# A two-MLP kernel: one VectorE pass less in the first activation, the second MLP's weight decoding spread over the first, block sums moved to VectorE

## Chip, cores and metric

The kernel runs on one core of a Trainium2 chip (trn2). The metric is the device time of one execution in microseconds (us), lower is better; the median of several runs is given where there are several. The engines are TensorE (PE in the rows, its weight loads PEld), VectorE (DVE), ScalarE (ACT), GpSimd (POOL) and SyncE (SP), which here only issues DMAs.

## What is computed

Attention over x and 32 state rows per head gives 544 rows for each of 8 batches, 4352 rows of 512 (64 x 8 heads). They go through two MLPs, each 512 to 2048 to 512. The weights arrive as float64, the rest as float32.

```python
def _moe_ref(x, w_in, w_out):            # first MLP
    h = x @ w_in
    g = np.where(h >= 1, h, np.where(h <= -1, 0.0, (h + 1) ** 2 / 4))
    return g @ w_out

def _moe2_ref(x, w_in, w_out, alpha):    # second MLP
    h = x @ w_in
    g = np.maximum(h, 0.0) + alpha * np.minimum(h, 0.0)
    return g @ w_out
```

## The kernel before

**Weights.** TensorE multiplies in float32 or in a rounded format (fp32r). A float32 operand is split into a rounded high part and the rest as a low part, and a product is three matmuls (high x high, high x low, low x high; `mm3`, and the loops of `out_mm`, `h_item`, `o_item`). The high part is a ScalarE copy (`hi_`, L73), the low part a subtraction (`lo_`, L76), on VectorE unless an engine is named. A float64 weight tile (512 KB) is loaded as raw words by `d_load` (L302) into a buffer of pool V and turned to float32 by integer work: `dec0` is one ScalarE operation (L309), `dec1` four VectorE operations (L318, L320, L323, L326), the last of which frees the V buffer. Pool V has 10 buffers of 4 KB a partition, pool U has 80 of 2 KB, and PSUM has 4 banks for accumulators and 4 for everything else.

**First MLP.** Nine tiles of columns: tiles 0 to 7 are the 512 rows of x of a batch, tile 8 (256 wide) the state rows. Each tile has 16 steps, one for each 128 hidden features, so `steps` has 144 entries and `gi(t, f)` numbers them. At step i the list `side[i]` (filled by `at`) holds the other work that is written there: attention of the next batch, loads, decoding. The main loop takes `g_split(i + 1)`, the side work, `h_mm(i + 2)` and `act_fn(i + 2)` together, one piece of each in turn (`run`), then `out_mm(i)`. The weights of the first layer differ by tile: `vr_load` (L426) fetches those of the next tile, two steps ahead of `vr_hi`. Tile 8 takes the plain weights, which `w1s_load` (L450) fetches in 32 transfers of 256 KB.

**Activation.** `act_fn` has ScalarE write y = relu(h/2 + 1/2) from PSUM (L488), VectorE g = max(h, y) from PSUM (L489), then in a later piece VectorE g = min(y, 1) * g (L491). The PSUM bank of h is free after L489.

**Second MLP.** `second()` runs units q of 7 products (`h_item`, L668): block sums of activations and weights replace 8 products by 7. `w_sums` (L569) makes four sums of weight blocks a unit, `w_split` their high and low parts, `h_after` and `slope` (L693, L679) combine the products and apply the activation on VectorE and ScalarE. From the 36th product on, an output item (`o_split`, `o_item`, L733) stands after about every 1.75 products; its weights `wv` are loaded by `wo_get` (L653). `x_prep` builds the sums and splits of the activations for the next group of rows along one unit in eight; its low parts are half on GpSimd. GpSimd also runs `w_sums`, two of the four low parts in `w_split`, every second low part of `o_split`, and the low part of `w2o_put`.

**Second MLP's weights.** The 16 input tiles (`w2i`) are loaded, decoded and stored again (`w2i_store`, L548) from step `gi(6, 8)` on, one each 1.2 steps. The 16 output tiles (`w2o`) are decoded inside `second()`: the dictionary `later` places load, `dec0`, `dec1`, `w2o_put` (split) and `w2o_store` (L607) by product number, one tile each 1.75 products from product 24 on.

**Order.** The code's order gives priorities; a scheduler then fixes one order of instructions for each engine, and each engine (and SP's queue of DMAs) works through its own strictly in order, waiting where an input or a free buffer is not there yet.

Of the kernel before, what the change touches and what calls it, by code (L numbers as in the profile page):

```python
# [13 lines left out]
AF = mybir.ActivationFunctionType  # L14
# [26 lines left out]
def kernel_body(ctx: ExitStack, tc: tile.TileContext, x, state, w1i, w1o, w2i, w2o, alpha, out):  # L41
# [440 lines left out]
    def act_fn(i):  # L482
        n = wd_(steps[i][0])
        ps = HP.pop(i)[:, :n]
        g = U(f"g{i}")
        GG[i] = g
        y = U(f"y{i}")
        act.activation(out=y[:, :n], in_=ps, func=AF.Relu, bias=0.5, scale=0.5)  # L488
        dve.tensor_tensor(out=g[:, :n], in0=ps, in1=y[:, :n], op=ALU.max)  # L489
        yield  # L490
        dve.scalar_tensor_tensor(out=g[:, :n], in0=y[:, :n], scalar=1.0, in1=g[:, :n],  # L491
                                 op0=ALU.min, op1=ALU.mult)

# [66 lines left out]
    def w_sums(q):  # L560
# [6 lines left out]
        for o, a, b, op in ((s1, a21, a22, ALU.add), (s2, s1, a11, ALU.subtract),  # L567
                            (s3, a11, a21, ALU.subtract), (s4, a12, s2, ALU.subtract)):
            pool.tensor_tensor(out=o, in0=a, in1=b, op=op)  # L569
            yield  # L570

    def w_split(q, n):
# [9 lines left out]
        yield  # L582
        lo_(l, t, h, pool if n % 2 else dve)
        if n == 0:
# [11 lines left out]
    def w2o_put(n):  # L596

        raw = G.pop(("dec", ("w2o", FO[n])))
        h, l = U(f"woh{n}", F32R), U(f"wol{n}", F32R)
        hi_(h, raw)  # L600
        WR["o", n] = h, l
        yield
        lo_(l, raw, h, pool)

# [108 lines left out]
    def o_split(m):  # L713
# [5 lines left out]
        hi_(h, g)  # L719
        lo_(l, g, h, pool if m % 2 else dve)  # L720
        GS[m] = (h, l)
# [30 lines left out]
    def second():  # L752
# [7 lines left out]
        for kind, n in ev:  # L760
            if kind == "h":
                q, k = divmod(n, 7)
                h_item(n)
                h_after(n)
                todo = later.pop(n, [])
                if k == 0 and q + 2 < NL // 7:
# [89 lines left out]

    for n in range(16):
        key = ("w2i", n // 2, n % 2)
        o = gi(6, 8) + int(1.2 * n)
        at(o - 3, d_load, key, src_w2p(*key[1:]))  # L860
        decode(key, o)
        at(o + 5, w2i_store, *key[1:])
    later = defaultdict(list)
    for n, f in enumerate(FO):
        key = ("w2o", f)
        o = 24 + int(1.75 * n)
        later[o - 6].append((d_load, key, src_w2o(f)))
        later[o - 1].append((dec0, key))
        later[o].append((dec1, key))
        later[o + 2].append((w2o_put, n))  # L870
        later[o + 5].append((w2o_store, n))
    for k in range(4):
# [90 lines left out]
```

## Time and profile before

| what | value |
|---|---|
| median of 3 runs | 1567.62 us (1563.13 to 1568.17) |
| the profiled execution | 1563.17 us |
| its span, first to last instruction | 1561.4 us |
| mean granted TensorE clock | 0.961 |
| PE / DVE / ACT / POOL busy | 1442.1 / 1050.0 / 692.6 / 469.7 us |

The span is the time between the first and the last instruction; 1.8 us of the execution lie around it. Busy time of an engine is the time in which it had an instruction; the share of the span hides that the program has stages with different limits, so it is read stage by stage. A low granted clock follows where TensorE has been waiting.

### The profile page before, as it was taken

Reading aid. Unit: us, or ns where it says so; the run is one execution under the profiler, and the core shown is the slowest. Engines: PE = TensorE matmul, PEld = TensorE weight load, DVE = VectorE, ACT = ScalarE, POOL = GpSimd, SP = SyncE. Lnnn points to the kernel's source line nnn. Section 1 sums busy time; section 2 is a strip of 40 time slices with the busy share of each in tenths; the row PEclk is TensorE's granted clock in tenths of the full one; section 3 lists DMA queues with packets and bytes.
Section 4 is the critical chain, followed back from the end, with each engine's and each line's share of the span. In section 5 each row is a group of like instructions: output and inputs, shape, how many; then the busy total and the mean of one; then the engine's idle time right before and its main releaser. Section 6 shows DMA issues by size and latency. Waiting matters only on the chain.

```text
span 1561.4 us, 19131 instructions
## 1 busy us (share of the span) xinstructions
PE 1442.1 (92%) x6460; PEld 1182.7 (76%) x6460; DVE 1050.0 (67%) x1697; ACT 692.6 (44%) x1354; POOL 469.7 (30%) x461
## 2 busy tenths in 40 slices
PE   4599999999999999995797899999999999999997
PEld 2255688888888888785775677888788888878886
DVE  7798597868696879863379987445644665575530
ACT  3244565555544545432244444333434443444431
POOL 1112101121000000001255566434544554464521
PEclk8899999999999999997898999999999999999999
DMA  8999725565412214643334755344544554645554
GB/s 239 290 286 317 228 75 149 151 189 162 154 50 88 83 66 145 222 171 122 118 108 163 254 191 188 131 149 152 175 148 162 188 183 164 207 165 179 182 172 165
DMA packets 180090, 262.73 MB, mean 168 GB/s; under 512 B 76824, under 2 KB 88600, under 8 KB 179992
## 3 DMA queue, kind: packets, MB, share of 16 engines
q1 hardware_dynamic: 107720, 235.45, 44.8%
q0 software_dynamic: 66560, 17.01, 6.2%
q10 hardware_dynamic: 5712, 9.05, 1.6%
q8 instruction: 51, 0.84, 0.2%
q14 instruction: 47, 0.39, 0.1%
HBM read 205.66 MB, written 55.57 MB: 167 GB/s over the span
## 4 chain that ended last, share of the span: by engine, by line
PE 71%; DMA 12%; DVE 10%; issue 2%; ACT 2%; POOL 1%; SPq 0%; ACTq 0%; DVEq 0%; POOLq 0%
PE accB L733 20%; PE accA L524 19%; PE hB L668 17%; PE hA L84 10%; DMA wr_wi<-in_moe_w_in_dram 2%; DMA wr_w1o<-in_moe_w_out_dram 2%; DMA vr<-vd 1%; DMA w1s33l<-wd 1%; PE accA L516 1%; PE sr L84 1%; DVE u L693 1%; PE sc L84 1%; DMA w1s13h<-wd 1%; DVE xt L634 1%; DMA w1s03l<-wd 1%
## 5 line engine op out<-in xcount | busy, mean ns | idle before, releaser
L733 PE MATMUL accB<-wv,gs 128*128 128x512 f32 x1632 | 406.7, 398 | 13.0 <-ACT gs L73 5.1
L733 PEld LDWEIGHTS accB<-wv,gs 128*128 128x128 f32 x1632 | 309.7, 191 | 78.1 <-ACT gs L73 6.4
L668 PE MATMUL hB<-xh,wh 128*128 128x384 f32 (+1 forms) x640 | 223.8, 371 | 24.3 <-DVE u L693 16.2
L668 PE MATMUL hB<-xl,wh 128*128 128x384 f32 (+1 forms) x560 | 205.0, 366 | 0.0
L489 DVE TENSOR_TENSOR g<-hA,y 128x512 f32<-128x512 f32 (+1 forms) x144 | 94.6, 657 | 146.9 <-ACT y L488 146.6
L668 PE MATMUL hB<-xh,wl 128*128 128x384 f32 (+1 forms) x480 | 175.1, 365 | 0.0
L668 PEld LDWEIGHTS hB<-xh,wh 128*128 128x128 f32 x640 | 122.7, 193 | 49.1 <-DVE u L693 23.6
L693 DVE TENSOR_TENSOR u<-hB,p 128x384 f32<-128x384 f32 (+1 forms) x80 | 48.6, 607 | 130.9 <-PE hB L668 121.2
L73 ACT CAST gh<-g 128x512 fp32r<-128x512 f32 (+1 forms) x128 | 76.1, 594 | 99.9 <-DVE g L491 92.8
L408 POOL DMA_DIRECT2D ws<-wd x64 | 51.2, 808 | 226.3 <-DMA wd<-w_wi_0l 31.0
L668 PEld LDWEIGHTS hB<-xl,wh 128*128 128x128 f32 x560 | 108.8, 194 | 12.5
L677 ACT ACTIVATE m<-u 128x384 f32<-128x384 f32 (+1 forms) x80 | 45.4, 568 | 155.6 <-DVE u L693 155.5
L488 ACT ACTIVATE y<-hA 128x512 f32<-128x512 f32 (+1 forms) x144 | 82.4, 572 | 40.3 <-PE hA L84 40.2
L491 DVE SCALAR_TENSOR_TENSOR g<-y,g 128x512 f32<-128x512 f32 (+1 forms) x144 | 99.0, 687 | 0.1
L668 PEld LDWEIGHTS hB<-xh,wl 128*128 128x128 f32 x480 | 92.4, 192 | 8.1
L76 DVE TENSOR_TENSOR gl<-g,gh 128x512 fp32r<-128x512 f32 (+1 forms) x128 | 86.6, 677 | 1.0 <-ACT gh L73 1.0
L76 POOL TENSOR_TENSOR gs<-u,gs 128x384 fp32r<-128x384 f32 (+1 forms) x40 | 45.3, 1132 | 127.7 <-ACT gs L73 127.7
L76 POOL TENSOR_TENSOR gs<-p,gs 128x384 fp32r<-128x384 f32 (+1 forms) x40 | 48.7, 1218 | 110.0 <-ACT gs L73 106.7
L679 DVE SCALAR_TENSOR_TENSOR u<-m,beta_sb,u 128x384 f32<-128x384 f32 (+1 forms) x80 | 61.6, 770 | 27.0 <-ACT m L677 26.3
L73 ACT CAST gs<-u 128x384 fp32r<-128x384 f32 (+1 forms) x80 | 44.4, 556 | 79.6 <-PE accB L733 78.5
L76 POOL TENSOR_TENSOR wl<-sb,wh 128x512 fp32r<-128x512 f32 x40 | 54.3, 1356 | 80.8 <-ACT wh L73 80.6
L76 POOL TENSOR_TENSOR xl<-xr,xh 128x384 fp32r<-128x384 f32 (+1 forms) x15 | 20.3, 1356 | 175.7 <-PE accA L524 166.6
(917 smaller groups left out, 3302.8 us busy)
## 6 DMA issues: line engine op xcount, KB each, us to landing
wv<-wod SPq DMA_DIRECT2D x160, 512.0 KB
wr<-wid SPq DMA_DIRECT2D x80, 256.0 KB
x<-in_x_dram SPq DMA_DIRECT2D x32, 512.0 KB
ws<-wd POOLq DMA_DIRECT2D x64, 256.0 KB, 11.8
vd<-vgo SPq DMA_DIRECT2D x64, 256.0 KB
vr<-vd SPq DMA_DIRECT2D x56, 256.0 KB
out_dram<-oB SPq DMA_DIRECT2D x34, 256.0 KB
wr_wi<-in_moe_w_in_dram SPq DMA_DIRECT2D x16, 512.0 KB
```

Of the source, the lines that this page charges most:

```text
L73: act.copy(h, raw)
L76: (eng or dve).tensor_tensor(out=l, in0=raw, in1=h.bitcast(F32), op=ALU.subtract)
L84: pe.matmul(ps, a, b, start=(k == 0), stop=(k == n - 1))
L408: pool.dma_start(out=t, in_=wd[blk][:, h * D:(h + 1) * D, :])
L488: act.activation(out=y[:, :n], in_=ps, func=AF.Relu, bias=0.5, scale=0.5)
L489: dve.tensor_tensor(out=g[:, :n], in0=ps, in1=y[:, :n], op=ALU.max)
L491: dve.scalar_tensor_tensor(out=g[:, :n], in0=y[:, :n], scalar=1.0, in1=g[:, :n], op0=ALU.min, op1=ALU.mult)
L524: pe.matmul(ACC[k][:, :n], a, b, start=(f == 0 and j == 0), stop=(f == NF - 1 and j == 2))
L668: pe.matmul(ps, a[:, kk], b, start=(p in (0, 5, 4) and m == 0), stop=(m == 5), skip_group_check=True)
L679: dve.scalar_tensor_tensor(out=g, in0=m, scalar=beta_sb[:, f:f + 1], in1=h, op0=ALU.mult, op1=ALU.add)
L693: dve.tensor_tensor(out=out, in0=a, in1=b, op=ALU.add)
L733: pe.matmul(OA[k], a, b, start=(r == 0 and j == 0), stop=(r == NF - 1 and j == 2))
```

## The change

Three edits. In `act_fn` ScalarE squares y in place after the Relu, and one VectorE operation makes g = max(min(y², 1), h), reading h from PSUM; it stands in the second piece, where L491 stood, so the bank of h is now free after it. The four block sums of `w_sums` and the low parts of `w_split`, `w2o_put` and `o_split` that were on GpSimd go to VectorE; `x_prep`'s stay on GpSimd. The second MLP's 32 weight tiles are all decoded along the first MLP, one each 3.2 steps from step `gi(1, 6)` to `gi(7, 9)`, and `later` is gone.

```diff
         y = U(f"y{i}")
         act.activation(out=y[:, :n], in_=ps, func=AF.Relu, bias=0.5, scale=0.5)
-        dve.tensor_tensor(out=g[:, :n], in0=ps, in1=y[:, :n], op=ALU.max)
-        yield
-        dve.scalar_tensor_tensor(out=g[:, :n], in0=y[:, :n], scalar=1.0, in1=g[:, :n],
-                                 op0=ALU.min, op1=ALU.mult)
+        act.activation(out=y[:, :n], in_=y[:, :n], func=AF.Square)
+        yield
+        dve.scalar_tensor_tensor(out=g[:, :n], in0=y[:, :n], scalar=1.0, in1=ps, op0=ALU.min, op1=ALU.max)
...
-            pool.tensor_tensor(out=o, in0=a, in1=b, op=op)
+            dve.tensor_tensor(out=o, in0=a, in1=b, op=op)
...
-        lo_(l, t, h, pool if n % 2 else dve)
+        lo_(l, t, h)
...
-        lo_(l, raw, h, pool)
+        lo_(l, raw, h)
...
-        lo_(l, g, h, pool if m % 2 else dve)
+        lo_(l, g, h)
...
-                todo = later.pop(n, [])
+                todo = []
...
-    for n in range(16):
-        key = ("w2i", n // 2, n % 2)
-        o = gi(6, 8) + int(1.2 * n)
-        at(o - 3, d_load, key, src_w2p(*key[1:]))
+    w2 = [("w2i", n // 2, n % 2) for n in range(16)] + [("w2o", f) for f in FO]
+    for n, key in enumerate(w2):
+        o = gi(1, 6) + int(3.2 * n)
+        at(o - 3, d_load, key, src_w2p(*key[1:]) if key[0] == "w2i" else src_w2o(key[1]))
         decode(key, o)
-        at(o + 5, w2i_store, *key[1:])
-    later = defaultdict(list)
-    for n, f in enumerate(FO):
-        key = ("w2o", f)
-        o = 24 + int(1.75 * n)
-        later[o - 6].append((d_load, key, src_w2o(f)))
-        later[o - 1].append((dec0, key))
-        later[o].append((dec1, key))
-        later[o + 2].append((w2o_put, n))
-        later[o + 5].append((w2o_store, n))
+        if key[0] == "w2i":
+            at(o + 4, w2i_store, *key[1:])
+        else:
+            at(o + 1, w2o_put, key[1])
+            at(o + 5, w2o_store, key[1])
```

How the order of instructions moves, at three places.

VectorE, a step of tile 3 (g50 is the activation of step 50; xt and xl are attention's). Before:

```order
L489 TENSOR_TENSOR g50_3014<-hA32_2991,y50_3015 128x512
L76 TENSOR_TENSOR gl49_3010<-g49_2961,gh49_3009 128x512
L142 STREAM_TRANSPOSE xt401_3019<-x1_40_2908 128x4x4x32
L491 SCALAR_TENSOR_TENSOR g50_3014<-y50_3015,g50_3014 128x512
L76 TENSOR_TENSOR xl400_3024<-xt400_3012,xh400_3022 128x512
L489 TENSOR_TENSOR g51_3065<-hA33_3044,y51_3066 128x512
```

and with the change:

```order
L76 TENSOR_TENSOR gl49_3092<-g49_3039,gh49_3091 128x512
L142 STREAM_TRANSPOSE xt401_3101<-x1_40_2981 128x4x4x32
L492 SCALAR_TENSOR_TENSOR g50_3096<-y50_3097,hA32_3072 128x512
L76 TENSOR_TENSOR xl400_3106<-xt400_3094,xh400_3104 128x512
L318 TENSOR_SCALAR wf_w2i_4_1_3143<-wf_w2i_4_1_3143 128x512
L76 TENSOR_TENSOR gl50_3146<-g50_3096,gh50_3145 128x512
```

L489 is gone, the one operation on g50 stands where L491 stood, and a piece of decoding (L318) has come in.

SP's queue of DMAs, late in tile 7 (w1s are tile 8's first-layer weights, wr_w2o the raw output weights of the second MLP, wid the stores of decoded input weights, wod those of split output weights, wv their loads for the first output items). Before:

```order
L450 DMA w1s00h_6201<-wd0_91 128x1x512
L450 DMA w1s00l_6202<-wd0_91 128x1x512
L548 DMA wid_89<-wf_w2i_6_0_6123 128x512
L302 DMA wr_w2o_0_7442<-in_moe2_w_out_dram 128x512
L548 DMA wid_89<-wf_w2i_6_1_6163 128x512
L450 DMA w1s01h_6243<-wd0_91 128x1x512
L450 DMA w1s01l_6244<-wd0_91 128x1x512
L302 DMA wr_w2o_1_7454<-in_moe2_w_out_dram 128x512
```

and with the change:

```order
L426 DMA vr731_6357<-vd1_3_87 128x1x512
L653 DMA wv2_7900<-wod_90 128x1024
L450 DMA w1s00h_6430<-wd0_91 128x1x512
L450 DMA w1s00l_6431<-wd0_91 128x1x512
L607 DMA wod_90<-woh14_6439 128x512
L607 DMA wod_90<-wol14_6440 128x512
L450 DMA w1s01h_6469<-wd0_91 128x1x512
L450 DMA w1s01l_6470<-wd0_91 128x1x512
```

The loads and stores of decoding between the w1s transfers are fewer, and three wv loads, which need V buffers, stand ahead of the first w1s.

VectorE in the second MLP, around unit 18 (wl, wh: low parts for unit 19; gs: low parts for output items). Before:

```order
L693 TENSOR_TENSOR u2_18_10179<-hB185_10172,p1_18_10166 128x384
L76 TENSOR_TENSOR wh190_10211<-wr190_10005,wh190_10211 128x256
L76 TENSOR_TENSOR wl192_10214<-sa19_10181,wh192_10213 128x512
L76 TENSOR_TENSOR gs56_10266<-u2_12_9113,gs56_10266 128x512
L693 TENSOR_TENSOR u3_18_10241<-hB185_10172,p1_18_10166 128x384
```

and with the change:

```order
L693 TENSOR_TENSOR u2_18_10179<-hB185_10172,p1_18_10166 128x384
L569 TENSOR_TENSOR sa19_10181<-wr190_10005,wr191_10007 128x2x128
L569 TENSOR_TENSOR sb19_10182<-wr190_10005 128x2x128
L569 TENSOR_TENSOR sa19_10181<-sa19_10181,wr190_10005 128x2x128
L76 TENSOR_TENSOR wh190_10211<-wr190_10005,wh190_10211 128x256
L569 TENSOR_TENSOR sb19_10182<-wr191_10007,sa19_10181 128x2x128
L76 TENSOR_TENSOR wl192_10214<-sa19_10181,wh192_10213 128x512
L76 TENSOR_TENSOR gs56_10266<-u2_12_9113,gs56_10266 128x512
L76 TENSOR_TENSOR gs57_10303<-u3_12_9175,gs57_10303 128x512
L693 TENSOR_TENSOR u3_18_10241<-hB185_10172,p1_18_10166 128x384
```

Between u2 and u3 of a unit stand now eight operations instead of three.

## Rows read from the trace of the kernel before

**Rows 1.** Busy time of each engine by stretch (us; x: instructions).

```profile
core 0: us, PE busy (x) PEld busy (x) DVE busy (x) ACT busy (x) POOL busy (x), PEclk, DMA share, GB/s
0.00:200.00 200.00, 154.36 (x489) 94.69 (x490) 151.97 (x288) 91.79 (x174) 32.15 (x48) 0.91 0.97 271
200.00:600.00 400.00, 399.99 (x1846) 331.87 (x1845) 315.45 (x534) 213.69 (x414) 37.50 (x42) 1.00 0.39 114
600.00:640.00 40.00, 40.00 (x184) 33.00 (x183) 39.58 (x81) 23.94 (x49) 0.00 (x0) 1.00 0.58 191
640.00:690.00 50.00, 48.56 (x213) 39.64 (x213) 41.51 (x73) 20.14 (x36) 0.00 (x0) 1.00 0.65 213
690.00:787.00 97.00, 70.99 (x440) 65.64 (x438) 35.02 (x69) 25.96 (x60) 19.66 (x17) 0.82 0.37 131
787.00:820.00 33.00, 30.55 (x130) 23.93 (x131) 25.48 (x36) 16.03 (x31) 18.96 (x18) 1.00 0.20 63
820.00:960.00 140.00, 116.39 (x439) 87.77 (x438) 126.42 (x152) 64.19 (x118) 89.18 (x68) 0.90 0.58 199
960.00:1080.00 120.00, 120.00 (x531) 99.26 (x530) 60.34 (x83) 44.82 (x80) 45.53 (x45) 1.00 0.44 149
1080.00:1120.00 40.00, 37.16 (x166) 31.42 (x165) 28.46 (x38) 19.18 (x40) 26.32 (x24) 0.96 0.44 152
1120.00:1240.00 120.00, 120.00 (x590) 106.94 (x589) 62.59 (x96) 46.10 (x92) 55.37 (x56) 1.00 0.52 173
1240.00:1280.00 40.00, 36.31 (x163) 31.88 (x162) 27.53 (x43) 20.69 (x45) 24.62 (x24) 0.91 0.53 179
...
1360.00:1400.00 40.00, 36.28 (x161) 31.69 (x160) 30.06 (x44) 19.75 (x43) 25.68 (x24) 0.91 0.46 158
```

**Rows 2.** VectorE's groups, 200 to 690 us: form and count, busy us, mean ns, idle before.

```profile
L491 DVE SCALAR_TENSOR_TENSOR g<-y,g 128x512 f32<-128x512 f32 x107 | 77.0, 719 | 0.0
...
L489 DVE TENSOR_TENSOR g<-hA,y 128x512 f32<-128x512 f32 x106 | 72.7, 686 | 68.7 <-ACT y L488 68.4
```

**Rows 3.** ScalarE's groups, 200 to 600 us.

```profile
L73 ACT CAST gh<-g 128x512 fp32r<-128x512 f32 x85 | 52.8, 622 | 53.8 <-DVE g L491 52.9 <-ACT oA L534 0.8
L488 ACT ACTIVATE y<-hA 128x512 f32<-128x512 f32 x85 | 50.7, 597 | 12.7 <-PE hA L84 12.6
```

**Rows 4.** VectorE's groups, 600 to 690 us.

```profile
L323 DVE SCALAR_TENSOR_TENSOR wf_w2i<-wr_w2i,wf_w2i 128x512 int32<-128x512 int32 x16 | 10.9, 683 | 0.2
...
L318 DVE TENSOR_SCALAR wf_w2i<-wf_w2i 128x512 f32<-128x512 f32 x15 | 6.2, 420 | 4.0 <-ACT wf_w2i L309 4.0
...
L76 DVE TENSOR_TENSOR xsl<-xsf,xsh 128x256 fp32r<-128x256 f32 x4 | 1.7, 419 | 0.0
```

**Rows 5.** The chain that ended last, 600 to 820 us (start, length, what).

```profile
641.08 10.82 DMA vr<-vd
...
746.79 17.77 DMA w1s33l<-wd
```

**Rows 6.** SP's DMA issues, 615 to 800 us (start, length, what).

```profile
662.78 0.54 SPq L450 DMA_DIRECT2D w1s00h<-wd  x1
...
687.07 0.59 SPq L450 DMA_DIRECT2D w1s10h<-wd  x1
...
746.79 4.36 SPq L450 DMA_DIRECT2D w1s33l<-wd  x1
```

**Rows 7.** VectorE's groups, 820 to 960 us.

```profile
L323 DVE SCALAR_TENSOR_TENSOR wf_w2o<-wr_w2o,wf_w2o 128x512 int32<-128x512 int32 x16 | 20.2, 1261 | 0.4
...
L679 DVE SCALAR_TENSOR_TENSOR u<-m,beta_sb,u 128x512 f32<-128x512 f32 x12 | 11.7, 976 | 2.3 <-ACT m L677 2.1
```

**Rows 8.** What TensorE waited for, 960 to 1560 us (total us, times, longest).

```profile
PE hB L668 <- DVE u L693: 10.0, 6, 2.8
```

**Rows 9.** GpSimd's groups, 1120 to 1240 us.

```profile
L76 POOL TENSOR_TENSOR wl<-wr,wh 128x512 fp32r<-128x512 f32 x7 | 9.1, 1294 | 0.0
...
L569 POOL TENSOR_TENSOR sa<-sa,wr 128x256 f32<-128x256 f32 x7 | 6.5, 931 | 0.0
```

## The prediction, made before the changed kernel ran

> **What bounds the kernel now.** I read the busy time by stretch first, then in each stretch with a gap the waits and the chain, then the groups of VectorE, ScalarE and GpSimd for prices. From 200 to 640 us TensorE is busy for the whole stretch at full clock, and so it is from 960 to 1080 and from 1120 to 1240 us [rows 1]: there only TensorE's own work counts. In 960 to 1080 us a matmul takes 120/531 = 0.226 us, in 1120 to 1240 us 120/590 = 0.203 us (fewer columns); these two paces say what a stretch would take without gaps. The gaps are in four places. (a) The first 200 us, with DMA at 0.97 of its engines' time. (b) 690 to 787 us, tile 8: clock 0.82, and the chain there is a row of w1s transfers, the last of which lands 17.8 us after its issue [rows 5], at 746.8 + 17.8 = 764.6 us. (c) 787 to 960 us: 130 + 439 = 569 matmuls [rows 1], worth 569 x 0.226 = 129 us in a stretch of 173 us, so 44 us are lost. VectorE is busy for 126.4 of the 140 us from 820 on. (d) Three short stretches where `x_prep` runs: 166, 163 and 161 matmuls in 40 us each [rows 1]. At 0.215 (the mean of both paces), 0.203 and 0.203 us they are worth 35.6, 33.2 and 32.7 us, so 4.4, 6.8 and 7.3 us are lost, 18.5 together.
>
> **Activation, tiles 0 to 7.** Out go 128 passes of 0.686 us on VectorE (and 16 half-wide ones in tile 8) [rows 2]; the pass that stays is of the form that took 0.719. In come as many squares on ScalarE. No row shows a square; its nearest rows are the Relu of the same line, 0.597, and a copy from SBUF, 0.622 [rows 3]. I take 0.622, the copy, since the square reads SBUF too. In 200 to 600 us that is 85 x 0.622 = 53 us on top of ScalarE's 213.7 [rows 1, 3], two thirds of 400: it lies beside TensorE's work. What it costs is time in which a bank of h is held: it is freed by an operation that stands where L491 stood, two or three VectorE operations of about 0.69 us later than L489, some 1.5 to 2 us. With four banks and a step of 490/107 = 4.6 us [rows 2] that is cover for most steps, less in tiles 2 and 3, where a second bank or a third is taken in each step.
>
> The Trainium skill, "ScalarE: Activation LUTs", section "Rules for kernel authors", speaks against this part: it wants max, min and mul on VectorE, which it calls up to about three times faster per element (for single-source bf16). Were a square three times 0.686 us, ScalarE would need some 389 us of those 400 before any decoding, and with the decoding just over 400; an estimate by the page's factor is then about 8 us over the first MLP, 1535 instead of 1527. The rows do not agree for these float32 tiles (0.597 and 0.622 on ScalarE against 0.686 on VectorE), so the sum goes by the rows.
>
> **Decoding moved into tiles 1 to 7.** One tile costs VectorE twice 0.683 and twice 0.420 us [rows 4], 2.2 us, and each 3.2 steps take 14.7 us, so 400 us hold 27 tiles, 60 us; some eleven of them are output tiles with one more low part of 0.69. VectorE in 200 to 600 us comes to 315.5 - 85 x 0.686 + 60 + 8 = 325 of 400 us. That TensorE stands this is shown by 600 to 640 us, where decoding already runs at one tile each 1.2 steps: VectorE busy 39.6 of 40 us, TensorE 40.0 [rows 1]. So VectorE and ScalarE cost nothing here. The DMAs may: each decoded tile brings a load of 512 KB and stores of 256 or 512 KB into SP's queue, ahead of the loads `vr` of the next weights, which have two steps, 9.2 us. In the stretch where before has such a mixture one `vr` took 10.8 us [rows 5], and 640 to 690 us shows 48.56 busy of 50 us [rows 1], 1.4 us lost. The rate is now lower, 2.7 times fewer tiles for the same time. Bounds: 0, and 1.4 us for each of the 28 weight blocks (four in each of seven tiles), 40 us. I take 4 us, near the lower end, since 600 to 640 us lost nothing at a higher rate.
>
> **The first 200 us.** About 16 passes of 0.686 us leave VectorE, 11 us; but three raw loads of the second MLP now come in at its end, 1.5 MB at the 271 GB/s of that stretch [rows 1], 6 us, and it is DMA that is full. I take 0, bounds -6 and +6.
>
> **Tile 8.** The 32 w1s transfers are issued from 662.8 us on, the ninth at 687.1, the last at 746.8 [rows 6]: after the ninth one each 59.7/23 = 2.6 us, and 24.3 us for the first eight, because raw loads and stores stand between them. Without those, eight take 21 us. But now wv2 stands in front of w1s00h in SP's queue. Of the ten V buffers three hold xsf, xsh and xsl, four xr, and the last three the raw tiles 13 to 15, so wv2 waits for the last decoding at `gi(7, 9)`, two steps (9 us) after the place of the first w1s. Bounds: the stream starts as before and keeps 2.6 us each, so that it lands 16 us earlier; or it starts 9 us later and gains 3, 6 us later. I take -4 us, a little over half way to the earlier end: the wait is for the last raw tile alone, and the whole stream gains from an emptier queue.
>
> **Second MLP, 787 to 960 us.** The decoding goes, and with it four VectorE operations, one of GpSimd and three DMAs for each of 16 tiles. L323 takes 1.261 us here against 0.683 in 600 to 690 us, where GpSimd is idle, and L679 0.976 [rows 4, 7]: beside GpSimd VectorE's operations stretch. What is left on VectorE for a unit is less than in 960 to 1080 us, where it is busy half the time. So most of the 44 us go. I leave 3.6 us of the start (33 - 130 x 0.226) and 6.2 us, the mean of the three losses under (d), for the `x_prep` that lies in this stretch too: -34.6 us. Bounds: -44 and -24, if VectorE's new work (below) keeps ten.
>
> **Work from GpSimd to VectorE, 960 us on.** Per unit four sums (0.419 us each, the row of that size without GpSimd), two low parts and two of `o_split` at 0.69: 4.4 us in 23 to 30 us, where VectorE is half busy [rows 1]; GpSimd took 0.931 and 1.294 us for them [rows 4, 9], and its stretching of the others goes. In full stretches nothing changes. Under (d) TensorE waits for `h_after`'s sums (10.0 us directly, six waits [rows 8]), which stand behind `x_prep` in VectorE's queue. There VectorE gets 4 to 5 us more to do and loses about as much stretching; a round trip over GpSimd falls away. I take -2 us, bounds -18.5 and +8.
>
> **Sum.** 1563.2 + 4 + 0 - 4 - 34.6 - 2 = 1526.6, so **1527 us**. The profiled execution is 4.4 us under the median of 1567.6 shown; the comparison is with that median, so 1527 means 2.6% less.
>
> **Rivals.** *More than that:* the stretches under (d) close for good and the w1s stream isn't held up: 16.5 and 12 us beyond my terms, 1499 us. For it: GpSimd's slow operations leave these stretches. Against it: VectorE's queue is what TensorE waits for, and it gets longer. *Given back in part:* raw loads crowd the tiles, and about half of the 28 blocks lose 1.4 to 2 us: some 25 us instead of 4, 1548 us; for it the 10.8 us landing, against it 200 to 600 us, with DMA at 0.39 [rows 1]. *Slower:* SP's queue. A raw load that finds no free V buffer holds everything behind it, `vr` among it. Each block late costs TensorE its lateness. From 40.6/28 = 1.45 us a block on, the gain is gone; at 2.2 us the time is 1523 + 62 = 1585 us. For it: 32 more V loads in tiles 1 to 7, in order, for ten buffers. Against it: in 600 to 640 us the same loads came 2.7 times as often and nothing was lost. That the change doesn't move the decoding is excluded: SP's order has the raw loads from tile 0's end on.
>
> **How the numbers follow.** A difference under 0.3% can't be told from none here. My forecast (1513 to 1541) gets 0.55, more 0.16, part given back 0.18, slower 0.11. Of the part given back 0.05 may end within 0.3% of before. So faster 0.84, same 0.05, slower 0.11. The range leaves out the slower case and the far end of the other two: 1500 to 1556.
>
> **What would show it.** Right: TensorE full from 200 to 640 us; w1s33l landing 0 to 10 us earlier relative to tile 7's end; from tile 8's end on no gap of over 1 us before the first `x_prep`, and VectorE's L679 at 0.69 to 0.75 us; short gaps at the later `x_prep`s. Wrong: TensorE waiting for hA or `vr` in tiles 1 to 7, SP waiting at L302 with `vr` behind it, or VectorE over 90% busy in the second MLP's full stretches with TensorE waiting for u.

## The result and the profile after

The changed kernel takes **1503.69 us** (median of 4 runs, 1502.98 to 1505.79) against 1565.38 us before (4 runs beside it): ratio 0.961, interval 0.9583 to 0.9637. The forecast was 1527 us, range 1500 to 1556. The direction and the large term were right; 62 us went where 40 were forecast. The profiled execution took 1504.31 us, its span 1502.5 us.

Busy time by stretch of the changed kernel (us; x: instructions), which answers to [rows 1]:

```profile
core 0: us, PE busy (x) PEld busy (x) DVE busy (x) ACT busy (x) POOL busy (x), PEclk, DMA share, GB/s
0.00:140.00 140.00, 97.28 (x297) 56.80 (x298) 112.07 (x226) 68.69 (x128) 24.53 (x41) 0.90 1.02 283
140.00:160.00 20.00, 10.71 (x37) 7.20 (x36) 5.15 (x9) 5.84 (x12) 2.12 (x3) 0.81 1.02 295
...
260.00:280.00 20.00, 13.49 (x58) 10.58 (x57) 7.17 (x12) 8.88 (x17) 1.56 (x2) 0.83 0.65 180
280.00:640.00 360.00, 360.00 (x1664) 300.28 (x1663) 284.52 (x506) 257.98 (x481) 29.79 (x34) 1.00 0.58 175
640.00:690.00 50.00, 50.00 (x223) 41.39 (x222) 28.87 (x47) 30.75 (x53) 0.00 (x0) 1.00 0.41 146
690.00:780.00 90.00, 71.58 (x462) 65.41 (x461) 35.41 (x62) 35.31 (x80) 8.53 (x7) 0.89 0.32 114
...
820.00:960.00 140.00, 138.64 (x610) 113.60 (x609) 108.10 (x179) 60.84 (x111) 10.17 (x7) 1.00 0.40 138
960.00:1050.00 90.00, 90.00 (x399) 74.53 (x398) 57.99 (x99) 33.58 (x60) 2.04 (x2) 1.00 0.44 148
1050.00:1090.00 40.00, 39.41 (x189) 34.27 (x188) 33.01 (x58) 20.89 (x42) 5.67 (x5) 1.00 0.54 186
...
1180.00:1220.00 40.00, 39.54 (x195) 34.89 (x194) 34.80 (x66) 21.79 (x47) 7.73 (x7) 1.00 0.50 182
...
1310.00:1350.00 40.00, 39.52 (x194) 34.72 (x193) 34.31 (x64) 21.51 (x47) 7.73 (x7) 1.00 0.56 194
```

Read it against [rows 1] from the bottom up. The three `x_prep` stretches (the rows of 40 us from 1050 on) have TensorE busy for 39.4 to 39.5 us, where it was 36.3 to 37.2: these gaps closed. 820 to 960 us has 138.6 of 140 busy, where it was 116.4: the large gap closed. 690 to 780 us still loses 18 us. Two gaps are new: 140 to 160 and 260 to 280 us.

The activation's prices, in the groups of 200 to 690 us on VectorE:

```profile
L492 DVE SCALAR_TENSOR_TENSOR g<-y,hA 128x512 f32<-128x512 f32 x105 | 71.2, 679 | 33.2 <-ACT y L490 32.9
```

and on ScalarE:

```profile
L490 ACT ACTIVATE y<-y 128x512 f32<-128x512 f32 x105 | 66.3, 632 | 2.9
```

A square takes 0.632 us (0.622 was taken for it), the pass that stays 0.679 us.

Where the time went is seen best by when the two programs reach the same place. The table gives the start of a tile of the first MLP (its first output matmul), the first product of the second MLP, its 600th matmul (about where `x_prep` and the large gap end) and the end of the span, as differences in us from the profile of before (185.0, 703.5, 777.4, 963.4 us; span 1561.4). For the 600th, matmuls of products and of output items are counted together; the first 600 hold 396 of products in every kernel. The other rows are the experiments.

| kernel | median us, ratio [interval] | tile 1 | tile 8 | first product | 600th | end |
|---|---|---|---|---|---|---|
| changed | 1503.69, 0.961 [0.9583, 0.9637] | +4.6 | +8.5 | -2.2 | -41.7 | -58.9 |
| e1_act | 1560.73, 0.9982 [0.9967, 0.9997] | +6.6 | +2.2 | -0.5 | -2.0 | -3.0 |
| e2_decode | 1546.71, 0.9886 [0.9868, 0.9905] | +2.6 | +22.4 | +12.2 | -14.3 | -17.0 |
| e3_pool | 1532.31, 0.9799 [0.9782, 0.9815] | -0.6 | +0.3 | -0.5 | -12.7 | -30.9 |
| e4_late | 1504.66, 0.9625 [0.9602, 0.9648] | +4.5 | +7.6 | -0.6 | -41.8 | -58.4 |
| e5_junk | 1569.28, 1.0048 [1.0032, 1.0065] | +4.9 | +9.2 | -1.6 | -12.7 | +5.3 |
| e6_sums | 1516.92, 0.971 [0.9695, 0.9724] | +5.0 | +9.4 | -1.5 | -37.0 | -46.2 |
| e6_lows | 1512.87, 0.967 [0.9653, 0.9688] | +5.3 | +9.8 | -1.2 | -35.7 | -50.3 |
| e8_all | 1503.89, 0.963 [0.9614, 0.9646] | +6.5 | +10.6 | +0.1 | -39.4 | -57.4 |
| f3_x2pool | 1493.39, 0.9562 [0.9548, 0.9577] | +0.7 | -3.6 | -14.6 | -52.9 | -71.0 |
| f7_w1sact | 1494.2, 0.9548 [0.9531, 0.9564] | +3.3 | -0.5 | -8.1 | -47.9 | -65.9 |
| f8_w1s4 | 1472.26, 0.9411 [0.939, 0.9432] | +1.6 | +0.8 | -32.0 | -74.9 | -92.6 |
| f6_w1s | 1469.38, 0.9394 [0.9376, 0.9411] | +2.2 | -2.1 | -35.9 | -77.5 | -94.8 |

### The profile page after: what moved, and what is told of

Read it like the earlier page. It is cut to its first block, busy times and chain, and to the rows that moved or that the text cites. A ratio compares the mean times of both kernels' runs of the same rounds, so it can differ in the third digit from the quotient of the medians.

```text
span 1502.5 us, 18956 instructions
## 1 busy us (share of the span) xinstructions
PE 1410.2 (94%) x6460; PEld 1166.7 (78%) x6460; DVE 1045.4 (70%) x1889; ACT 782.5 (52%) x1498; POOL 111.2 (7%) x125
## 4 chain that ended last, share of the span: by engine, by line
PE 80%; DMA 10%; DVE 7%; ACT 2%; issue 1%; SPq 0%; POOL 0%; ACTq 0%; DVEq 0%; POOLq 0%
PE accB L733 22%; PE accA L524 21%; PE hB L668 20%; PE hA L84 11%; DMA wr_wi<-in_moe_w_in_dram 2%; DMA x<-in_x_dram 2%; DMA wr_w1o<-in_moe_w_out_dram 2%; PE accA L516 1%; PE sr L84 1%; PE sc L84 1%; DMA w1s33l<-wd 1%; DMA w1s13h<-wd 1%; DMA w1s23l<-wd 1%; DVE xl L76 1%; PE vgp L416 1%
## 5 line engine op out<-in xcount | busy, mean ns | idle before, releaser
L733 PE MATMUL accB<-wv,gs 128*128 128x512 f32 x1632 | 397.4, 391 | 0.2
L733 PEld LDWEIGHTS accB<-wv,gs 128*128 128x128 f32 x1632 | 305.1, 188 | 60.6 <-DVE gs L76 1.1
L668 PE MATMUL hB<-xh,wh 128*128 128x384 f32 (+1 forms) x640 | 217.9, 361 | 5.2 <-ACT p L697 2.9
L668 PE MATMUL hB<-xl,wh 128*128 128x384 f32 (+1 forms) x560 | 200.7, 358 | 0.0
L492 DVE SCALAR_TENSOR_TENSOR g<-y,hA 128x512 f32<-128x512 f32 (+1 forms) x144 | 93.6, 650 | 88.2 <-ACT y L490 87.7
L489 ACT ACTIVATE y<-hA 128x512 f32<-128x512 f32 (+1 forms) x144 | 82.6, 574 | 73.2 <-PE hA L84 73.2
L76 DVE TENSOR_TENSOR gs<-u,gs 128x384 fp32r<-128x384 f32 (+1 forms) x80 | 49.6, 621 | 69.5 <-ACT gs L73 69.2
L490 ACT ACTIVATE y<-y 128x512 f32<-128x512 f32 (+1 forms) x144 | 87.5, 608 | 4.2
L73 ACT CAST gs<-u 128x384 fp32r<-128x384 f32 (+1 forms) x80 | 44.4, 557 | 86.6 <-PE accB L733 85.5
L693 DVE TENSOR_TENSOR u<-hB,p 128x384 f32<-128x384 f32 (+1 forms) x80 | 48.6, 607 | 42.2 <-PE hB L668 37.4
L516 PE MATMUL accA<-g,wf_w1o 128*128 128x512 f32 x128 | 62.9, 627 | 8.1 <-DVE g L492 8.1
L679 DVE SCALAR_TENSOR_TENSOR u<-m,beta_sb,u 128x384 f32<-128x384 f32 (+1 forms) x80 | 53.4, 668 | 23.0 <-ACT m L677 22.3
L419 ACT COPY vgo<-vgp 128x512 f32<-128x512 f32 x64 | 36.7, 588 | 46.8 <-PE vgp L417 45.3
```

The lines of the kernel that those rows point to most:

```text
L73: act.copy(h, raw)
L76: (eng or dve).tensor_tensor(out=l, in0=raw, in1=h.bitcast(F32), op=ALU.subtract)
L490: act.activation(out=y[:, :n], in_=y[:, :n], func=AF.Square)
L516: pe.matmul(ACC[k], w[:, k * 128:(k + 1) * 128], g, start=(f == 0), stop=(f == NF - 1))
L668: pe.matmul(ps, a[:, kk], b, start=(p in (0, 5, 4) and m == 0), stop=(m == 5), skip_group_check=True)
L679: dve.scalar_tensor_tensor(out=g, in0=m, scalar=beta_sb[:, f:f + 1], in1=h, op0=ALU.mult, op1=ALU.add)
```

## Experiments: the three parts alone

**e1_act**: before, with `act_fn` of the change alone (the first hunk of the diff).

> The kernel before with the activation edit alone. Theory A (each edit has its own place): the first MLP is bound by TensorE in tiles 1 to 7, so a pass less on VectorE gives nothing there and at most a few us in the first 200 us: 1558 to 1567 us. Rival B (the later release of the PSUM bank of h is what made the changed kernel lose 12 us by tile 3): 1570 to 1580 us, with gaps near 145 and 265 us.

Measured 1560.7 us, 0.2% less. A VectorE pass off a stretch that TensorE already fills gives next to nothing, as forecast. But tile 1 starts 6.6 us late: the new gap at 140 to 160 us belongs to this part.

**e2_decode**: before, with the moved decoding alone; `todo = []` and the new table of places.

> The kernel before with the moved decoding alone, GpSimd's part and the old activation kept. Theory A: the 40 us lost between 787 and 960 us mostly go, the losses at x_prep (18 us) stay, and the first MLP loses 10 to 20 us, since VectorE there comes to about 383 of 400 us: 1535 to 1550 us. Rival C (the x_prep gaps close because the decoding's DMAs and VectorE work are gone, not because of GpSimd): 1515 to 1525 us, with no gaps of 4 us and more at x_prep.

Measured 1546.7 us. From the first product to the 600th matmul it wins 28.9 us (12.2 to -16.7), the decoding's part of the large gap, and 10.2 us in tile 8; after the 600th 0.3 us, so the gaps at `x_prep` stay. But it comes to tile 8 22.4 us late, more than the 10 to 20 expected, where the whole change loses 8.5. Tile 2 accounts for little of that difference: it lasts 89.7 us here, 87.6 in the whole change, 79.5 before (the gap at 260 us, next section). The difference lies in tiles 1 and 4 to 6, which together last 303.4 us here, 290.2 in the whole change and 291.4 before. One stretch of them, with the moved decoding alone:

```profile
505.00:585.00 80.00, 78.74 (x354) 63.07 (x353) 74.03 (x126) 44.16 (x84) 10.38 (x7) 1.00 0.41 134
```

and before:

```profile
505.00:585.00 80.00, 80.00 (x372) 66.64 (x371) 63.10 (x108) 39.24 (x76) 2.63 (x2) 1.00 0.21 73
```

With the pass that the activation edit takes out still there, VectorE is busy 74 of 80 us; TensorE waits 1.3 us and does 354 matmuls instead of 372. So the activation edit, worth next to nothing by itself, is the room into which the decoding moves: 303.4 against 290.2 us. That the room is VectorE's time is argued from these rows.

**e3_pool**: before, with GpSimd's sums and low parts on VectorE alone.

```diff
-            pool.tensor_tensor(out=o, in0=a, in1=b, op=op)
+            dve.tensor_tensor(out=o, in0=a, in1=b, op=op)
...
-        lo_(l, t, h, pool if n % 2 else dve)
+        lo_(l, t, h)
```

(and the two others of the diff).

> The kernel before with GpSimd's block sums and low parts on VectorE alone. Theory A: the x_prep gaps (4, 7 and 7 us) close and the start of the second MLP gains some 5 to 10 us while the decoding stays in it: 1537 to 1550 us. Rival C: the gaps stay, and VectorE, 90% busy there with the decoding, gets more to do: 1560 to 1575 us.

Measured 1532.3 us, better than expected: 13.0 us from the first product to the 600th matmul and 17.4 us after it, where the forecast had 2 us and the whole change wins 17.4. The gaps at `x_prep` close by this part alone.

## Experiments: the two new gaps in the first MLP

In the changed kernel TensorE waits there for these (total us, times, longest), at 140 to 160 and at 260 to 280 us:

```profile
PE vgp L416 <- DVE g L492: 9.3, 1, 9.3
...
PE accA L524 <- ACT gh L73: 6.5, 1, 6.5
```

ScalarE's timeline at the first of them (start, length, what, idle before):

```profile
143.34 0.60 ACT L489 ACTIVATE y<-hA 128x512 f32<-128x512 f32 x1
156.17 1.04 ACT L73 CAST x2h<-x 128x1024 fp32r<-128x1024 f32 x1 [12.23 <-DMA x<-in_x_dram]
157.12 0.62 ACT L490 ACTIVATE y<-y 128x512 f32<-128x512 f32 x1
```

Between the Relu and the square of one step stands the high part of attention's second copy of x (`x2h`), whose load was issued at 142.88 us and lands 13.2 us later. The square, L492 and the release of h's bank stand behind it. Before, the same cast waited too:

```profile
145.51 0.60 ACT L488 ACTIVATE y<-hA 128x512 f32<-128x512 f32 x1
154.03 1.04 ACT L73 CAST x2h<-x 128x1024 fp32r<-128x1024 f32 x1 [7.92 <-DMA x<-in_x_dram]
```

but behind it stood nothing of that step's activation, since after the Relu all was VectorE's.

**e4_late**: the changed kernel, decoding from tile 2 on, `o = gi(2, 10) + int(2.5 * n)`.

> The changed kernel with the decoding started 20 steps later (step gi(2,10), one tile each 2.5 steps). Theory D (the first MLP's two gaps near 145 and 265 us come from raw weight tiles that hold V buffers, so that attention's x is loaded late and ScalarE stands on it): both gaps go or shrink to what before had, 1490 to 1497 us. Rival B (the later release of the PSUM bank): the gaps stay, 1502 to 1506 us.

Measured 1504.7 us: missed. It is the number that rival B gave, and at the first gap TensorE does wait for a bank that L492 frees late; the next run shows that the cast is what makes it late. The first gap stays (it is not the raw loads'). The second goes: tile 2 lasts 79.3 us, as before (79.5), and the loss moves with the decoding to tile 3, 86.6 us against 79.6. In the changed kernel SP stands 11.6 us at a store of a decoded tile (L548, issued at 258.96 us, when L326 on that tile has ended), and the x2 load stands behind it, issued at 260.27 us; ScalarE then stands 8.70 us on the cast. e2_decode has the same gap with the old activation (8.26 us on the cast). So the second gap comes with the moved decoding, by the same cast. What of it is the queue is not separated: before, that load was issued at 260.28 us too, and the cast waited 2.82 us.

**f3_x2pool**: the changed kernel, x2's cast on GpSimd.

```diff
-        hi_(h2, a["x2"])
+        pool.tensor_copy(out=h2, in_=a["x2"])
```

> The changed kernel with the cast of x2 (x2h, 12 of 128x1024, tiles 2 to 7) on GpSimd, which has little to do in the first MLP, in place of ScalarE. Theory Q (the two new stalls, at 140 to 160 us and 260 to 280 us, are ScalarE's queue standing on that cast while the load of x2 is under way, with the activation's square behind it): PE keeps 19.5 of 20 us in both stretches, tile 1 begins as early as before (185 us), tile 2 some 10 us earlier than in the changed kernel, and the run takes 1490 to 1497 us. Theory R (the x2 load itself is late for its own consumer, the sum over x2 on PE, or GpSimd's cast holds the loads of ws that GpSimd issues behind it): the stalls stay or move to PE's wait for those, 1500 to 1510 us.

Measured 1493.4 us. The two stretches, as in the changed kernel's rows above:

```profile
140.00:160.00 20.00, 20.00 (x69) 12.62 (x68) 10.09 (x18) 10.29 (x20) 5.89 (x7) 1.00 0.93 287
260.00:280.00 20.00, 20.00 (x92) 16.55 (x91) 16.09 (x27) 13.15 (x24) 5.21 (x6) 1.00 0.83 234
```

Both stretches are full, and tile 8 starts 3.6 us earlier than before instead of 8.5 later. The loads are no earlier in the program (the second is issued at 256.37 us, with tile 2 starting at 260.2; 260.27 and 264.1 in the changed kernel). The wait has moved to GpSimd, which has little behind it that is due, but not nothing: it stands 28.01 us on the first cast, the loads of `ws` that it issues come behind, and TensorE waits 5.2 us for them:

```profile
160.00:180.00 20.00, 14.77 (x42) 8.38 (x41) 3.18 (x5) 8.69 (x17) 6.86 (x8) 0.86 1.11 235
```

Theory Q holds, with this part of theory R beside it.

## Experiments: what GpSimd's work cost

**e5_junk**: the changed kernel, and GpSimd repeats its old work into a spare tile that nobody reads.

```diff
             dve.tensor_tensor(out=o, in0=a, in1=b, op=op)
+            pool.tensor_tensor(out=parts(stT['t'][:, :512])[:, :, 0], in0=a, in1=b, op=op)
...
         lo_(l, g, h)
+        if m % 2:
+            lo_(stT['t'][:, :w], g, h, pool)
```

(the same for `w_split`'s odd low parts).

> The changed kernel, in which GpSimd again does in the second MLP what it did before (the four block sums of a unit, the odd low parts of the weights and of the outer product's operand), but into a spare tile that nobody reads; VectorE makes the results that count, as in the changed kernel. GpSimd's late results are thus out of the chain, its work beside VectorE is back. Theory X (the link: what cost time before was that sums and low parts came late out of GpSimd): no change, 1500 to 1508 us, and the x_prep stretches keep PE at 39 of 40 us. Theory Y (the stretching: VectorE's own operations take longer while GpSimd works, a low part 1.25 us against 0.55, L679 0.82 against 0.61, and the PSUM bank of hB comes free late): the x_prep stretches fall back to about 35 of 40 and the run gives back 10 to 20 us, 1513 to 1524 us. As a control it also holds a small real link: a buffer comes free only when GpSimd's copy of the work has read it.

Measured 1569.3 us: 65.6 us given away, more than either theory had. VectorE's groups from 960 to 1480 us show how (busy us, mean ns). Before:

```profile
L679 DVE SCALAR_TENSOR_TENSOR u<-m,beta_sb,u 128x384 f32<-128x384 f32 (+1 forms) x59 | 43.0, 728 | 21.2 <-ACT m L677 20.7
...
L693 DVE TENSOR_TENSOR u<-hB,u 128x384 f32<-128x384 f32 (+1 forms) x58 | 33.9, 584 | 6.6 <-PE hB L668 5.6
L76 DVE TENSOR_TENSOR gs<-u,gs 128x384 fp32r<-128x384 f32 (+1 forms) x30 | 31.6, 1054 | 12.5 <-ACT gs L73 12.5
...
L76 DVE TENSOR_TENSOR wl<-sa,wh 128x512 fp32r<-128x512 f32 x29 | 21.8, 753 | 27.7 <-ACT wh L73 27.7
```

The changed kernel:

```profile
L76 DVE TENSOR_TENSOR gs<-u,gs 128x384 fp32r<-128x384 f32 (+1 forms) x65 | 39.2, 603 | 56.2 <-ACT gs L73 55.8
L679 DVE SCALAR_TENSOR_TENSOR u<-m,beta_sb,u 128x384 f32<-128x384 f32 (+1 forms) x58 | 37.0, 637 | 16.0 <-ACT m L677 15.6
L693 DVE TENSOR_TENSOR u<-hB,u 128x384 f32<-128x384 f32 (+1 forms) x58 | 33.4, 576 | 1.6 <-PE hB L668 0.7
...
L76 DVE TENSOR_TENSOR wl<-sa,wh 128x512 fp32r<-128x512 f32 x28 | 19.3, 688 | 0.9
...
L76 DVE TENSOR_TENSOR wl<-wr,wh 128x512 fp32r<-128x512 f32 x28 | 19.2, 684 | 0.0
```

e5_junk (L682 and L696 are L679 and L693, three lines further down):

```profile
L76 DVE TENSOR_TENSOR wl<-wr,wh 128x512 fp32r<-128x512 f32 x28 | 49.8, 1780 | 0.0
L76 DVE TENSOR_TENSOR gs<-u,gs 128x384 fp32r<-128x384 f32 (+1 forms) x58 | 46.4, 807 | 7.7 <-ACT gs L73 5.5 <-issue 2.2
L682 DVE SCALAR_TENSOR_TENSOR u<-m,beta_sb,u 128x384 f32<-128x384 f32 (+1 forms) x55 | 42.0, 764 | 18.6 <-ACT m L680 17.5
...
L696 DVE TENSOR_TENSOR u<-hB,u 128x384 f32<-128x384 f32 (+1 forms) x56 | 32.5, 581 | 0.8
```

With GpSimd idle a weight's low part takes 0.684 us, with GpSimd at work 1.780; the outer product's low part 0.603 against 0.807 (before 1.054, where GpSimd had every second one). L693 keeps its 0.58 us in all three. The difference between the lines is their operands: `m` and `u`, `wr` and `wh` lie in SBUF, `hB` in PSUM. L679 itself bears it out: its form with `hB` (`m<-m,beta_sb,hB`, 128x384) takes 0.606 us in the changed kernel and 0.601 here, its form `u<-m,beta_sb,u` 0.614 and 0.768. The Trainium skill, "SBUF — State Buffer", section "SBUF: two separate sides", has this rule: VectorE and GpSimd share a pair of SBUF ports under an exclusive lock, and a VectorE operation with two SBUF inputs takes part in it when GpSimd reads SBUF. These rows agree, 0.684 to 1.780 us for two SBUF operands and 0.576 to 0.581 for one. Two SBUF operands are not the only case, though: the decoding's L318 and L320 have one, and take 0.420 and 0.418 us at 600 to 690 us, with GpSimd idle, but 0.713 and 0.853 us at 820 to 960 us in the kernel before.

What this adds up to is seen in the busy time from 960 to 1480 us (columns as above), in the kernel before, the changed kernel and e5_junk:

```profile
960.00:1480.00 520.00, 509.75 (x2399) 445.20 (x2398) 294.34 (x436) 215.72 (x435) 253.63 (x252) 0.98 0.50 169
960.00:1480.00 520.00, 518.47 (x2492) 454.74 (x2491) 358.08 (x669) 219.37 (x442) 23.17 (x21) 1.00 0.52 179
960.00:1480.00 520.00, 497.11 (x2314) 428.07 (x2313) 472.54 (x641) 202.01 (x416) 280.02 (x244) 0.98 0.47 163
```

GpSimd's work beside VectorE, with no reader for its results, is thus enough to take back the whole gain: VectorE is busy 472.54 us for fewer matmuls. But this does not measure what before lost. VectorE does all the work here as well; before, it was busy only 294.34 us, less than in the changed kernel. And some buffers come free here only when GpSimd has read them.

**e6_sums** and **e6_lows**: the changed kernel with the sums alone, or the odd low parts of the weights and of the outer product alone, back on GpSimd (`dve` to `pool` in `w_sums`; `pool if n % 2 else dve` and its like in the other two).

> The changed kernel with the four block sums of a unit alone back on GpSimd, whose results are used; the low parts stay on VectorE. GpSimd then works 4 times 0.93 us a unit, half of what it did before. Theory X (the link: the chain sums, cast on ScalarE, low part on VectorE is late, and VectorE's in-order queue stands on it): nearly all of what moving GpSimd's work gave comes back, 1514 to 1524 us, with VectorE waiting for ScalarE's casts of sa and sb. Theory Y (the stretching): about half of it, in the x_prep stretches only, 1506 to 1514 us.

> The changed kernel with every second low part (two of a unit's four weight low parts, every second one of the outer product's operand) back on GpSimd, results used; the block sums stay on VectorE. Per unit that is about 4.8 us of GpSimd's work, against 3.7 us in the run with the sums back, which gave 13 us away. Theory Y (stretching: VectorE's operations with two SBUF operands take longer while GpSimd works): 1515 to 1526 us, low parts on VectorE at 0.9 us or more, while VectorE's operations that read PSUM (u<-hB, 0.607 us) keep their time. Theory X (only a late result in the chain costs): each low part is at most 0.6 us later than on VectorE and nothing waits for it in the full stretches: 1503 to 1509 us.

Measured 1516.9 and 1512.9 us, 13.2 and 9.2 us given back. The first lies in theory X's range, the second between the two ranges. For the low parts the rows point to lengthening, and no wait of another engine is put down to GpSimd; of VectorE's groups from 960 to 1480 us (e6_lows),

```profile
L679 DVE SCALAR_TENSOR_TENSOR u<-m,beta_sb,u 128x384 f32<-128x384 f32 (+1 forms) x58 | 42.1, 727 | 20.1 <-ACT m L677 19.3
...
L693 DVE TENSOR_TENSOR u<-hB,u 128x384 f32<-128x384 f32 (+1 forms) x58 | 33.4, 576 | 3.0 <-PE hB L668 2.1
...
L76 DVE TENSOR_TENSOR gs<-u,gs 128x384 fp32r<-128x384 f32 (+1 forms) x31 | 27.7, 892 | 24.3 <-ACT gs L73 24.2
```

0.637 becomes 0.727 and 0.603 becomes 0.892, though less of the time is lost than theory Y had put on it. For the sums it is more than that. They keep GpSimd busy for less time (113 us of 960 to 1480 us, against 169 with the low parts), yet cost more, and VectorE's groups of e6_sums in the `x_prep` stretch at 1200 to 1220 us, where TensorE is busy 16.1 of 20 us, show both:

```profile
L76 DVE TENSOR_TENSOR xl<-xr,xh 128x384 fp32r<-128x384 f32 x2 | 2.7, 1364 | 0.0
...
L76 DVE TENSOR_TENSOR wl<-sa,wh 128x512 fp32r<-128x512 f32 x1 | 0.7, 692 | 2.7 <-ACT wh L73 2.7
```

a lengthened operation (1.364 us), and VectorE standing 2.7 us for the cast of a sum that came late out of GpSimd, with `h_after`'s sums behind it. Neither theory holds alone here; how the 13.2 us divide was not separated.

**e8_all**: `x_prep`'s low parts on VectorE as well, `lo_(l, src, h)`.

> The changed kernel with x_prep's low parts, the last work of GpSimd in the second MLP (15 of 128x384 or 128x512 at 1.25 us on GpSimd), on VectorE too. Theory Y (stretching): VectorE gains about 1 us of work (0.55 to 0.65 us each) per low part and loses the lengthening beside it; since PE already keeps 39.5 of 40 us in these stretches, at most 2.5 us in all are to be had: 1500 to 1504 us. Theory Z (VectorE becomes the bound in the x_prep stretches, where it is busy 31 to 35 of 40 us): 1505 to 1515 us.

Measured 1503.9 us, no difference: what is left of GpSimd's work lies where TensorE has hardly a gap to close (39.4 to 39.5 of 40 us busy).

## Experiments: the stream of tile 8's weights

After f3_x2pool the largest gap left is 690 to 780 us. There SP issues a w1s every 2.4 us:

```profile
722.10 2.38 SPq L450 DMA_DIRECT2D w1s31h<-wd  x1
724.53 2.44 SPq L450 DMA_DIRECT2D w1s31l<-wd  x1
```

and these rows show the loss and the low share of DMA (second last column):

```profile
690.00:780.00 90.00, 69.39 (x449) 63.52 (x448) 37.08 (x66) 33.60 (x80) 9.37 (x7) 0.87 0.35 125
705.00:735.00 30.00, 20.91 (x151) 19.71 (x150) 14.21 (x23) 11.46 (x29) 3.82 (x3) 0.83 0.27 103
```

**f6_w1s** and **f7_w1sact**: f3_x2pool, the low half of each w1s from GpSimd's queue, or from ScalarE's: `(pool if k else ld).dma_start(...)`, `(act if k else ld).dma_start(...)`.

> The run with x2's cast on GpSimd (1493 us), and on top the 16 low halves of tile 8's weights (w1s..l) issued from GpSimd's queue in place of SP's. In that run 690 to 780 us has TensorE busy 69.4 of 90 us, and SP issues a w1s each 2.4 us with the DMA engines busy 0.26. Theory P (one queue's pace of 256 KB each 2.4 us is the limit): two queues halve the stream, most of the 20.6 us lost there close, 1474 to 1483 us. Theory S (the transfer itself is the limit, in what it reads from or writes to, or GpSimd's queue is slower than SP's): 1490 to 1500 us with the same gaps.

> As the run before, with the low halves issued from ScalarE's queue in place of GpSimd's. Theory P: 1474 to 1483 us as well, if ScalarE's own in-order queue does not stand on the free buffers of the transfers; theory R (ScalarE's casts and activations of tile 7 stand behind an issue that waits for a free U buffer, and TensorE waits for gh): 1485 to 1500 us. Theory S as before: 1490 to 1500 us.

Measured 1469.4 and 1494.2 us. A second queue helps if it is GpSimd's, and not at all if it is ScalarE's. In f6_w1s:

```profile
705.00:735.00 30.00, 29.28 (x242) 28.88 (x241) 20.30 (x35) 16.32 (x41) 9.07 (x9) 1.00 0.53 120
```

In f7_w1sact:

```profile
705.00:735.00 30.00, 19.91 (x125) 18.50 (x124) 11.94 (x21) 9.44 (x23) 2.57 (x2) 0.76 0.28 110
```

Two queues, and the share of DMA is 0.28 as with one: SP's packets take 0.131 of the engines' time and ScalarE's 0.150, where SP's alone took 0.257. TensorE waits 15.3 us at 690 to 780 us for low halves of w1s and 3.5 us for gh, so theory R explains the smaller part at most. A second queue by itself does not lift the limit. The Trainium skill, "DMA: Bandwidth & Descriptors", section "Why a DMA increments its semaphore by 16 and not by 1", offers a cause: a transfer is spread over the largest number of engines, up to 16, that divides the outermost dimension of both its source and its destination, for SP and ScalarE always the lowest-numbered ones, for GpSimd (below 16) a run of them that moves on. The source of a w1s has 4 outermost (`h e i` with h = 4); an estimate by that page is 4 of 16, 0.25. The shares agree (0.27, 0.28, and 0.53 with GpSimd's queue); which engines worked, no run here shows.

**f8_w1s4** tests that with SP's queue alone.

```diff
-            ld.dma_start(out=t.bitcast(F32), in_=src.rearrange("(h e i) f -> h e i f", h=4, e=2)[:, c % 2])
+            for h4 in range(4):
+                o = 64 * h4 + 32 * (c % 2)
+                ld.dma_start(out=t.bitcast(F32)[32 * h4:32 * h4 + 32], in_=src[o:o + 32])
```

> The run with x2's cast on GpSimd (1493 us), with every w1s transfer of 256 KB (4 blocks of 32 rows) issued as four of 64 KB (32 rows each), all from SP's queue. Theory K (what limits the stream is that a transfer whose outermost dimension is 4 is spread over four DMA engines, always the same ones for SP and ScalarE: that fits a share of 0.26, and ScalarE's queue bringing nothing): with 32 outermost rows a piece the share of DMA rises above 0.4 though the queue is the same, and the gaps at 700 to 780 us close: 1468 to 1480 us. Theory P (the pace belongs to the queue, 256 KB each 2.4 us, or more issues make it slower): the gaps stay or grow, 1490 to 1515 us.

Measured 1472.3 us, and in the same stretch:

```profile
705.00:735.00 30.00, 27.34 (x224) 26.79 (x223) 18.89 (x31) 16.90 (x42) 6.43 (x5) 1.00 0.52 152
```

One queue, the same bytes, four times as many issues, and the share is 0.52 instead of 0.27. The last w1s is there 15.6 us after its issue in f3_x2pool (issued at 734.5 us, first used at 750.1) and 2.0 us after it here (731.2 and 733.2). That is what theory K forecast, and theory P is out. What is shown is that the pace hangs on how the transfers are cut; that more engines work is the page's account of it. f6_w1s and f8_w1s4 both beat the changed kernel, by 2.2% and 2.0% of the time before, of which 0.5% is the cast on GpSimd; their intervals overlap.

## Why the prediction was right or wrong

By the terms of its sum, on the profiled executions (differences of the table's columns):

| term | forecast | measured |
|---|---|---|
| first 200 us | 0 | +4.6 |
| decoding in tiles 1 to 7 | +4 | +3.9 |
| tile 8 | -4 | -10.7 |
| 787 to 960 us | -34.6 | -39.3 |
| GpSimd's work and `x_prep`, from 960 us on | -2 | -17.4 |

The forecast's terms come to -36.6 us on the profiled execution; against the median shown, 1567.6 us, that read as 40.6. The measured 1503.7 us lies outside the forecast's own band, 1513 to 1541, and inside the stated range only in the part kept for the rival "More than that". Of the 22.3 us missed, 15.4 belong to the last term.

- **The large term was right in cause and nearly in size.** The step that bounded it (44 us lost at most, 3.6 and 6.2 left) came 4.7 us short. Alone, the moved decoding wins 28.9 us here (e2_decode) and GpSimd's work on VectorE 13.0 (e3_pool); together they win 39.3.
- **The step that failed is the last term**, "There VectorE gets 4 to 5 us more to do and loses about as much stretching; a round trip over GpSimd falls away", taken as -2 us. The first half was, if anything, too favourable: what VectorE gets to do outweighs the lengthening that goes. From 960 to 1480 us it is busy 358.08 us for 2492 matmuls, where it was 294.34 us for 2399 (a sum costs it 0.416 us and a low part 0.68; its own operations go from 1.054 to 0.603 and from 0.728 to 0.637 us). The gaps closed although its queue got longer. What decided was not how long VectorE is busy but how late its results come, and that second half was priced at next to nothing. Before, VectorE stood 27.7 us for casts of block sums that came out of GpSimd (`wl<-sa`), 2.0 to 2.7 us of it in each `x_prep` stretch, with `h_after`'s sums behind; with the change it stands 0.9 us. From the 600th matmul on, the sums alone back on GpSimd give back 8.9 of the 17.4 us, the low parts 5.4. How much of that is late results and how much operations lengthened in front of `h_after`'s sums stays open. The bound of -18.5 held. This was the rival "More than that", to which 0.16 was given, with 16.5 us beyond this term and 12 beyond tile 8's: 15.4 and 6.7 came. What was said against it, that VectorE's queue gets longer, was true and did not decide. The length of a unit in that step, 23 to 30 us, was too long: a product is 6 matmuls, and the changed kernel does 28 units in 520 us, 18.6 us each. That does not change the argument.
- **The first 200 us** failed in the step that costs the activation: "some 1.5 to 2 us" for the bank of h. It counted VectorE's operations up to the place of L491. But L492 also needs the square, and in front of the square the scheduler puts a cast on ScalarE that waits 12.2 us for a load. e1_act and f3_x2pool show it.
- **Tiles 1 to 7** came out right to 0.1 us by luck. `vr` was not late; 280 to 690 us has TensorE full. Tile 2 lost 8.1 us more than before, at the gap at 260 us, and 3.7 us came back in tiles 3 to 7, 2.5 of them in tile 7, where the kernel before decoded. SP's queue was held, as the rival "Slower" described, but it cost TensorE time once, not for 28 blocks, and what held it was the store of a decoded tile. The statement that "VectorE and ScalarE cost nothing here" holds only together with the activation edit (303.4 against 290.2 us in tiles 1 and 4 to 6).
- **Tile 8** was to be held up by wv2's wait for the last raw tile. That wait came: SP's waits from 659.5 to 668 us (total us, times, longest) and its issues in the changed kernel are

```profile
SPq L653 <- DVE wf_w2o L326: 6.9, 1, 6.9
...
667.28 0.32 SPq L653 DMA_DIRECT2D wv<-wod  x1
667.71 0.53 SPq L450 DMA_DIRECT2D w1s00h<-wd  x1
...
686.95 0.53 SPq L450 DMA_DIRECT2D w1s10h<-wd  x1
...
746.80 0.93 SPq L450 DMA_DIRECT2D w1s33l<-wd  x1
```

The stream starts 4.9 us later than before, and the first eight take 19.2 us, where it was 24.3 [rows 6], so the rest is issued when it was. The last one lands 15.9 us after its issue (17.8 before [rows 5]), 1.9 us earlier. Tile 7 ends 8.5 us later than before, so relative to it the stream ends 10.4 us earlier, close to the 10.7 measured. The step took this lateness of tile 7 for a term by itself, when tile 8's wait for the stream takes it up. Its bound of 16 us earlier does not follow from its figures: from 662.8 us, 31 steps of 2.6 us end at 743.4, 3.4 us earlier. The pace of 2.4 to 2.6 us after the eighth was taken as given; f8_w1s4 shows that cutting the transfers in another way changes it.

Sum: +4.6 + 3.9 - 10.7 - 39.3 - 17.4 = -58.9 us. The parts alone give 3.0 + 17.0 + 30.9 = 50.9. By the table, the whole change is 16.4 us better up to tile 8 than the three parts added up, 12.4 of them in tiles 1 to 7, where the activation edit makes room for the decoding; from tile 8 on it is 8.4 us worse than they are, which leaves the 8 us.

## What to carry to other kernels

Before two instructions of one chain are put on an engine that works strictly in order, look in its order at what the scheduler places between them: what counts is the latest input of anything in between, not the length of the operations. Look likewise at what stands behind the work on the engine that it is moved to. Elementwise work on GpSimd relieves VectorE by less than it seems, because VectorE's operations with two SBUF operands lengthen beside it; compare the mean of such a row in a stretch with GpSimd idle before you plan. And a result that comes late out of GpSimd can cost more than the time VectorE saves: here VectorE was busier without GpSimd and the gaps closed. When a stream of transfers leaves the DMA share near 0.25, try another shape of the transfer before adding queues.

## What the runs showed of the hardware that was not expected

A VectorE operation with two SBUF operands went from 0.684 to 1.780 us beside GpSimd's work, while one with an operand in PSUM stayed at 0.58 us. The decoding's operations with one SBUF operand went from 0.42 to 0.71 and 0.85 us beside GpSimd in the kernel before. A load of 4 blocks of 32 rows kept the DMA share at 0.27 from SP's queue and at 0.28 with half of it from ScalarE's; the same bytes as 32-row transfers from SP reached 0.52, and with half of them from GpSimd's queue 0.53.
